# Clustered attention and a mixture of experts on one core: 32-row transposes on VectorE, other operand parts, filler matmuls by plan, and new instruction orders

## The chip, the cores and the metric

The kernel runs on one core of one Trainium2 chip. The metric is device time in microseconds (us), as a median of repeated executions. Engines are named as in the profile: PE (TensorE, matrix products), PEld (its weight loads), DVE (VectorE), ACT (ScalarE), POOL (GpSimd) and SP (SyncE, whose queue issues every DMA of this kernel).

## The reference

Attention in which a query sees only the keys of its own cluster, then a layer in which every token takes the two best of four causal attention experts:

```python
# q, k, v: (4, 8, 768, 64); centroids: (8, 16, 64)
q_assign = np.argmax(np.einsum('bhsd,hcd->bhsc', q_n, c_n), axis=-1)   # q_n, k_n, c_n: rows of length 1
k_assign = np.argmax(np.einsum('bhsd,hcd->bhsc', k_n, c_n), axis=-1)
mask = q_assign[:, :, :, None] == k_assign[:, :, None, :]
scores = np.where(mask, scale * np.matmul(q, k.transpose(0, 1, 3, 2)), -1e9)
attn = np.exp(scores - scores.max(-1, keepdims=True))
x = attn / (attn.sum(-1, keepdims=True) + 1e-9) @ v     # heads side by side: (4, 768, 512)
logits = x @ w_gate                                     # the two best experts of a token, softmax w over them
for e in range(4):
    q, k, v = x @ wq[e], x @ wk[e], x @ wv[e]           # 64 columns each
    ...                                                 # causal softmax attention a
    out += (w where e was chosen) * (a @ v @ wo[e])
```

## The kernel before

The work is cut into 24 pairs `n`. Pairs 0 to 15 are the attention: a batch and two heads each. Pairs 16 to 23 are the experts: a batch and two experts each. A pair has two stages, operands (`attention_operands`, `moe_operands`) and `core`.

Operands of an attention pair. One DMA each brings `kt` and `qt` (L620; the profile shows every DMA at L468; runs of 1536 bytes in a partition). PE turns them in 128x128 blocks against the identity (`misc<-identf,kt`, L633), so that the partition holds the depth of even and of odd tokens, and ACT or DVE copies the result to `xk`, `xq`. They are split into a rounded part `hi` and a rest `lo`, so that products in the fast fp32r format keep their precision. Then the clusters are found:

- PE multiplies by the normalised centroids, four 32-row pieces side by side (L661), and the result (cluster in the partition, token in the column) is copied to `s` (L475).
- PE turns `s` in three 128x128 blocks (L670), so that a token's 16 products lie side by side.
- DVE finds the best of the 16 and makes the one-hot `oh` in five instructions of 384 columns (L676, L677, L678, L683, L684).
- PE turns `oh` back in three blocks (L692), and ACT makes the mask rows `rows` of it, with a scale and a bias that give 0 or -2^60 (L695). They go through DRAM (`rw`) into rows 64 to 79 of `tq` and `tk`.

`tk` and `tq` are the operands of the score products, with two slots of 128 rows each, filled by DMAs on SP (`put`, `put_last`): slot 0 has `hi` of K and of Q and the mask rows, slot 1 the crossing parts (`lo` of K with `hi` of Q, and the other way round). For pairs from 1 on, 63 of the 64 crossing rows lie in slot 1 and one row in row 96 of slot 0.

`core`. For each half of 384 queries: 12 row products per half over an 80-row slot (`row`, L1098; `st` for some of pair 0), of each of which DVE takes the largest element of a row (`mx<-row`, L1109). A small product turns the maxima (`misc<-identr,M`, L1121), ACT or DVE negates them into `mr`, and a DMA writes them as one more row of `tq` (`tq<-mr`, L1145). Then come the scores, two products each (`st`, L1180), the exponential on ACT (L1186), the product with V (`av`, L1225), and the sums of the exponentials, which POOL or DVE adds up (`acc`, L480 and L481) and PE reduces (L1251). 1/sum goes through DRAM to a broadcast tile `rb`, and the result to `xt` and to DRAM (`x`). The experts do the same with projections in place of loads (L857, L907, L1340).

What sets the order. Every step is an `op` with a number. The table `ORDER` lists the numbers for each engine, and `Plan.run` records the instructions in these orders, picking by an estimate of times which engine's next step comes first. So an engine's queue is fixed by the table, and each engine works its queue strictly in order. The table also says which of ACT, DVE and POOL does a copy or a sum that can run on two of them.

Filler. `spin` (L1355) is a product of ones, 256 columns of bf16, into the bank `av`. `Plan.run` puts it into gaps that it expects on PE, but only until the first real use of that bank. All 52 stand before the first `av` product.

Of the kernel before, what the change touches and what calls it, by code (L numbers as in the profile page):

```python
# [1409 lines left out]
```

## Time and profile before

| | us |
|---|---|
| median of 3 runs | 704.73 (704.49 to 705.03) |
| the profiled execution's own time | 706.39 |
| its span, first to last instruction | 704.6 |
| PE busy | 683.0, 97% of the span |
| DVE busy | 536.4, 76% |
| ACT, POOL busy | 396.3 (56%), 339.6 (48%) |
| mean granted PE clock | 0.988 |

The page gives each engine's busy time as a share of the span. A view of windows gives the same for a stretch of time, with the PE clock that was granted there (1.00 is full speed) and the mean share of the 16 DMA engines. A timeline lists instructions with start and duration, and in brackets how long the engine had been idle and what ended that. Matmuls overlap, so what one costs is read from the start of one to the start of the next, not from its duration.

### The profile page before, as it was taken

To read this page: it belongs to the slowest core of one execution; us is meant where nothing else is said; L and a number is where in the kernel's file an instruction comes from. 1 tells how busy PE (TensorE), PEld (TensorE's weight loads), DVE (VectorE), ACT (ScalarE), POOL (GpSimd) and SP (SyncE) were. 2 spreads that over 40 slices of the span, in tenths; PEclk is the share of its full clock that TensorE was granted. 3 is DMA by queue.
4 is the path that set the end of the run, shared out by engine and by line. 5 is a ranking of instruction groups with operands and counts; after the bars stand their busy time and mean duration, and the time that the engine had idled before them with its cause. 6 is when DMAs were issued, how large, how long until landed. Compare 5 with 4: busy or idle time off the path is not lost.

```text
span 704.6 us, 12566 instructions
## 1 busy us (share of the span) xinstructions
PE 683.0 (97%) x4204; PEld 512.4 (73%) x4204; DVE 536.4 (76%) x1127; ACT 396.3 (56%) x938; POOL 339.6 (48%) x281
## 2 busy tenths in 40 slices
PE   6899999999999999999999899989999999999997
PEld 4667667676766677767666588778967888897775
DVE  6898888787988788898788775676678488668842
ACT  6766757666675667757655554345355345343643
POOL 6726577685677356755555521643244101312520
PEclk9999999999999999999999899989999999999999
DMA  6876657567466466567565334253534446234322
GB/s 204 206 189 185 171 139 187 153 170 216 138 204 170 124 193 189 148 184 208 148 186 147 102 99 101 81 158 90 150 81 136 112 123 167 69 99 137 114 99 105
DMA packets 64871, 103.60 MB, mean 147 GB/s; under 512 B 22424, under 2 KB 39080, under 8 KB 64808
## 3 DMA queue, kind: packets, MB, share of 16 engines
q1 hardware_dynamic: 64808, 102.81, 52.9%
q8 instruction: 33, 0.54, 0.3%
q14 instruction: 30, 0.25, 0.1%
HBM read 39.49 MB, written 15.86 MB: 79 GB/s over the span
## 4 chain that ended last, share of the span: by engine, by line
PE 83%; DMA 8%; DVE 4%; ACT 2%; SPq 2%; issue 1%; POOL 1%; DVEq 0%; ACTq 0%
PE st L1180 23%; PE av L1225 20%; PE row L1098 13%; PE misc L857 9%; PE misc L907 5%; PE misc L1340 4%; PE misc L633 3%; PE misc L1251 2%; DMA tq<-mr 2%; DMA r<-sd 2%; SPq L468 2%; DVE acc L481 1%; DVE mx L1109 1%; PE misc L661 1%; DMA sd<-ssb 1%
## 5 line engine op out<-in xcount | busy, mean ns | idle before, releaser
L1109 DVE TENSOR_REDUCE mx<-row 128x1 f32<-128x384 f32 (+1 forms) x442 | 233.5, 549 | 58.9 <-PE row L1098 54.8
L1180 PE MATMUL st<-tq,tk 97*128 97x384 f32 (+4 forms) x1056 | 247.8, 342 | 3.0 <-DMA tq<-mr 1.8
L1180 PEld LDWEIGHTS st<-tq,tk 128*128 128x128 f32 (+1 forms) x1056 | 184.7, 193 | 18.1 <-issue 4.6
L1098 PE MATMUL row<-tk,tq 80*128 80x384 f32 (+3 forms) x506 | 173.0, 366 | 5.4 <-DVE mx L1109 3.7
L1098 PEld LDWEIGHTS row<-tk,tq 80*128 80x128 f32 x506 | 94.5, 193 | 46.7 <-DVE mx L1109 22.5
L1186 ACT ACTIVATE p<-st 128x384 f32<-128x384 f32 (+2 forms) x198 | 89.6, 477 | 58.9 <-PE st L1180 46.9
L1186 ACT ACTIVATE xh<-st 128x384 f32<-128x384 f32 x126 | 59.0, 492 | 35.8 <-PE st L1180 28.4
L1225 PE MATMUL av<-p,vt 128*64 128x384 f32 x308 | 56.4, 493 | 0.0
L1107 DVE TENSOR_TENSOR row<-row,tri 128x128 f32<-128x128 f32 x96 | 28.2, 294 | 34.1 <-PE row L1098 34.0
L1186 ACT ACTIVATE xl<-st 128x384 f32<-128x384 f32 x90 | 42.5, 489 | 14.2 <-PE st L1180 12.0
L480 POOL TENSOR_TENSOR acc<-acc,p 128x768 f32<-128x768 f32 (+1 forms) x18 | 33.2, 1846 | 33.7 <-ACT p L1186 15.9
L1225 PE MATMUL av<-xh,vt 128*64 128x384 f32 x252 | 45.6, 490 | 0.0
L1186 ACT ACTIVATE tk<-st 128x384 f32<-128x384 f32 (+2 forms) x66 | 27.2, 431 | 25.2 <-PE st L1180 24.9
L480 POOL TENSOR_TENSOR acc<-acc,xh 128x768 f32<-128x768 f32 x17 | 31.2, 1837 | 15.9 <-DVE acc L481 9.5
L1225 PEld LDWEIGHTS av<-p,vt 128*64 128x64 f32 x308 | 20.1, 136 | 25.4 <-issue 22.6
L480 POOL TENSOR_TENSOR lo<-xq,hi 128x384 fp32r<-128x384 f32 x23 | 23.6, 1039 | 28.0 <-DMA tk<-lo 17.3
L1302 POOL TENSOR_TENSOR xt<-avu,rb 128x384 f32<-128x384 f32 x28 | 29.0, 1046 | 12.3 <-DMA rb<-rd 9.8
L486 ACT ACTIVATE tk<-hi 64x768 fp32r<-64x768 f32 x39 | 32.8, 841 | 0.9 <-DVE hi L476 0.3
L1109 DVE TENSOR_REDUCE M<-row 128x1 fp32r<-128x512 f32 (+3 forms) x64 | 31.5, 492 | 2.2
L1225 PE MATMUL av<-xl,vt 128*64 128x384 f32 x180 | 33.1, 489 | 0.0
L1225 PEld LDWEIGHTS av<-xh,vt 128*64 128x64 f32 x252 | 17.2, 137 | 21.7 <-issue 21.3
L480 POOL TENSOR_TENSOR lo<-xk,hi 128x384 fp32r<-128x384 f32 x20 | 21.7, 1090 | 22.7 <-DMA tq<-lo 12.8
(300 smaller groups left out, 1381.9 us busy)
## 6 DMA issues: line engine op xcount, KB each, us to landing
tq<-hi SPq DMA_DIRECT2D x62, 192.0 KB
tk<-hi SPq DMA_DIRECT2D x46, 192.0 KB
tq<-lo SPq DMA_DIRECT2D x46, 192.0 KB
rb<-rd SPq DMA_DIRECT2D x46, 192.0 KB
vt<-in_v_dram SPq DMA_DIRECT2D x16, 384.0 KB
x<-xt SPq DMA_DIRECT2D x16, 384.0 KB
kt<-in_k_dram SPq DMA_DIRECT2D x15, 384.0 KB
qt<-in_q_dram SPq DMA_DIRECT2D x15, 384.0 KB
```

Source lines behind the costliest of these rows:

```text
L480: ways = [("pool", t_pool(n), lambda: POOL.tensor_tensor(dst(), a(), b(), op=fn)), ("dve", t_dve(n), lambda: DVE.tensor_tensor(dst(), a(), ...
L486: return op("act", t_act(n, True), lambda: ACT.activation(dst(), src(), AF.Copy), due, after, [use], alt=(MO["m_copy"], "pool", t_pool(n), ...
L857: PE.matmul(m()[:, :HW], w_[:, dc, es], x_[dc]()[:, c], start=(i == 0), stop=(i == 3 * DC - 1))
L907: PE.matmul(m()[:, :NV], x_[dc]()[:, ts], w_[:, dc, :], start=(i == 0), stop=(i == 3 * DC - 1))
L1098: PE.matmul(ps()[:, :w], cols(Q, slice(0, R), 0, h, hf, cc * 128, (cc + 1) * 128), by_head(K)[0:R, 0, h, i * w:(i + 1) * w] if moe else by ...
L1107: DVE.tensor_tensor(e, e, tri, op=OP.add)
L1109: DVE.tensor_reduce(to, ps()[:, :w], axis=AX.X, op=OP.max)
L1180: PE.matmul(p()[:, o_:HW], cols(K, rs, slot, h, kh, k0, k0 + 128), cols(Q, rs, slot, h, hf, o_, HW), start=(i == 0), stop=(i == 1))
L1186: ACT.activation(pt()[:, h, o_:HW], p()[:, o_:HW], AF.Exp, scale=SC)
L1225: PE.matmul(av()[h * 64:(h + 1) * 64, o_:HW], d["vv"](h, kc), pt()[:, h, o_:HW], start=(kc == 0), stop=(kc == nk - 1), tile_position=(0, 6 ...
L1302: e.tensor_tensor(xt().rearrange("d (p c t) -> d t c p", c=HC, t=2)[:, par], avu()[:, c].rearrange("d (c p) -> d c p", c=HC), rb()[:, c].r ...
L1340: PE.matmul(m(), a_()[:, ts], w_()[:, ep, :], start=(ep == 0 and i == 0), stop=(ep == EP - 1 and i == 2))
```

## The change

1. Both turns of the cluster step move from PE to DVE. DVE's transpose works within blocks of 32x32, so the layout is changed to suit it: the operands now have head and depth in the partition (no longer parity and depth), one centroid operand `cbd` for both heads of a pair with zeros where head and row don't match, and 32 rows of products for a piece. The products are turned from PSUM to PSUM (L692 of the new kernel), without the copy `s`; the one-hot `oh` is turned within SBUF to `ot` (L695), and ACT makes the mask rows from it (L714). Pair 0 does the step in two halves of 192 columns and writes its mask rows straight into `tk` and `tq` with ACT (L773), without a DMA.
2. The loads of K and Q become two DMAs each, one for a head, that write runs of 256 bytes. V's token order changes with it.
3. The crossing rows of every pair are now 32 rows in slot 0 and 32 in slot 1 (pair 0 had this before), so `put_last` goes. Counted in the built programs, SP issues 719 DMAs in place of 661: 32 more loads, 30 more operand parts, 4 fewer mask-row writes.
4. The filler has 128 columns, in the unused part of the bank `av`, and may stand anywhere that the plan expects a gap, with a running allowance of 0.7 us. There are 90 of them now: 70 before the first `av` product, 1 in the middle of the attention, 19 among the experts.
5. Constants that aren't needed at once are written later (`late_constants`), and the plan has other estimates for DMAs.
6. `ORDER` is new for all engines.

The same functions run on the engines otherwise. By the built programs DVE has 33 transposes more, and 5 sums of 768 columns, 4 of 384, 5 casts of 384 and 6 copies `ssb` fewer; POOL has 5 sums of 768 and 4 of 384 more.

```diff
-        o = op("pe", t_av(HW), go, c1 + 4, xs["k"] + xs["q"] + [cbd_ready], [m1, s_, x["k"], x["q"]], mode=32)
-        o = copy_op(s_, lambda: m1()[:, :HW], HW, c1 + 4.5, [o], [m1, s_])
...
-                PE.transpose(m2()[:, c * 128:(c + 1) * 128], s_()[:, c * 128:(c + 1) * 128], identf)
+        o = op("dve", t_dve(HW), lambda: DVE.transpose(m2()[:, :HW], m1()[:, :HW]), c1 + 4.5, [o], [m1, m2, oh, sm])
+
+        def turn_back(o, due, dst):
+            return op("dve", t_dve(HW), lambda: DVE.transpose(dst(), oh()), due, [o], [oh, dst])
...
-                PE.transpose(m4()[:, c * 128:(c + 1) * 128], oh()[:, c], identb)
-        o_r = op("act", t_act(HW) + 0.18, lambda: ACT.activation(
-            rows(), m4()[:, :HW], AF.Identity, scale=row_scale, bias=row_bias), c2 + 6.5, [o], [m4, rows])
+            o = turn_back(o, c2 + 3, ot)
+            o_r = op("act", t_act(HW, True) + 0.18, lambda: ACT.activation(
+                rows(), ot(), AF.Identity, scale=row_scale, bias=row_bias), c2 + 6.5, [o, late], [ot, rows])
...
-                dma(t().rearrange("p h c d -> p h (c d)"),
-                    src[b, 2 * pr:2 * pr + 2].rearrange("h (p c) d -> p h (c d)", c=NC))
+                        dma(t().rearrange("p (c h d) -> p h c d", c=NC, h=2)[:, h],
+                            src[b, 2 * pr + h].rearrange("(p c) d -> p c d", c=NC))
...
         for T, src, after in ((K, klo, los["k"]), (Q, qhi, his["q"])):
-            if n:
-                need_st += [put(T, slice(64, 127), 1, src, c2 + 0.8, after), put_last(T, src, c2 + 0.9, after)]
-            else:
-                need_st += [put(T, slice(96, 128), 0, src, c2 + 0.8, after),
-                            put(T, slice(64, 96), 1, src, c2 + 0.9, after, d0=32)]
+            need_st += [put(T, slice(96, 128), 0, src, c2 + 0.8, after),
+                        put(T, slice(64, 96), 1, src, c2 + 0.9, after, d0=32)]
...
-        top, mr_ = (0, 96) if moe else (1, 127 if n else 96)
+        top, mr_ = 0 if moe else 1, 96
...
+    REST, EASE = 0.7, 0.35
...
+                if self.start and not self.held:
+                    gap, dur = t - free["pe"], dur * self.pace(free["pe"])
+                    room = max(0.0, self.REST - self.rest)
...
+                    while mode == 128 and gap > max(room, 0.06) + dur:
                         f = Op("pe", dur, fn, 0.0, (), (), 0.0, 128, None, 0.0, False)
...
+                        self.rest = max(0.0, self.rest - self.EASE * dur)
+                    self.rest += max(gap, 0.0)
...
-        PE.matmul(idle()[:, :256], onesb, onesb[:, None, :].to_broadcast([128, 2, 128]), start=True, stop=True)
+        PE.matmul(avp[:, HW:], onesb, onesb, start=True, stop=True)
...
 ORDER = dict(
     pe="""
-6 4 11 9 1 181 0 18 179 186 20 184 193 23 195 346 56 48 50 54 64 348 46 62 60 52 58 351 66 353 68 74 198 360 80 71 76
+7 5 12 1 10 188 19 186 183 181 349 195 58 76 352 52 347 66 64 48 354 62 56 50 68 60 82 70 54 361 90 73 78 94 92 86 108
...
```

Three places in the queues, first of before and then of the change (a name's number is that of its buffer). The first is PE in the middle of the attention, from the centroid products of a pair (`misc<-xq,cbd`) on; before, PE turns their copy `s` three times a few products later, and `oh` some twenty rows further on.

```order
L661 MATMUL misc_2313<-xq_2170,cbd 32x384
L661 MATMUL misc_2313<-xk_2130,cbd 32x384
...
L1098 MATMUL row_2322<-tk_95,tq_96 128x384
L1180 MATMUL st_2329<-tq_100,tk_99 128x384 x2
L1098 MATMUL row_2335<-tk_95,tq_96 128x384
L670 MATMUL misc_2338<-identf,s_2327 128x128 x3
L1180 MATMUL st_2344<-tq_100,tk_99 128x384 x2
...
L1098 MATMUL row_2424<-tk_95,tq_96 128x384
L692 LDWEIGHTS oh_2411
L692 MATMUL misc_2426<-identb,oh_2411 128x128
...
L1098 MATMUL row_2431<-tk_95,tq_96 128x384
```

The same stretch of PE's queue with the change:

```order
L688 MATMUL misc_2292<-xq_2179,cbd 32x384
L688 MATMUL misc_2292<-xk_2008,cbd 32x384
...
L1129 MATMUL row_2300<-tk_86,tq_87 128x384
L1211 MATMUL st_2304<-tq_91,tk_90 128x384 x2
L1211 MATMUL st_2310<-tq_91,tk_90 128x384 x2
L1129 MATMUL row_2315<-tk_86,tq_87 128x384
L1211 MATMUL st_2317<-tq_91,tk_90 128x384 x2
L1129 MATMUL row_2323<-tk_86,tq_87 128x384
```

Both groups of turns have left PE; row and score products follow each other as before. The second place is DVE in the same pair: before, the two halves of the one-hot step (`sm`, `oh`), with the row maxima (`mx<-row`) and sums around them.

```order
L1109 TENSOR_REDUCE mx_2360<-row_2352 128x1
L1115 TENSOR_REDUCE M_102<-mx_2216 128x6
L676 TENSOR_REDUCE sm_2371<-misc_2338 128x24
L677 TENSOR_TENSOR misc_2338<-misc_2338,sm_2371 128x384
L678 TENSOR_TENSOR misc_2338<-misc_2338,ramp 128x384
L1109 TENSOR_REDUCE mx_2360<-row_2362 128x1
L481 TENSOR_TENSOR lo_2404<-xq_2170,hi_2320 128x384 x2
L481 TENSOR_TENSOR acc_0_2252<-acc_0_2252,p_0_2246 128x768
L683 TENSOR_REDUCE sm_2371<-misc_2338 128x24
L684 TENSOR_TENSOR oh_2411<-misc_2338,sm_2371 128x384
L1109 TENSOR_REDUCE mx_2360<-row_2414 128x1
```

The same step of DVE with the change:

```order
L1140 TENSOR_REDUCE mx_2228<-row_2315 128x1
L692 STREAM_TRANSPOSE misc_2331<-misc_2292 128x384
L1140 TENSOR_REDUCE mx_2228<-row_2323 128x1
L701 TENSOR_REDUCE sm_2345<-misc_2331 128x24
L702 TENSOR_TENSOR misc_2331<-misc_2331,sm_2345 128x384
L703 TENSOR_TENSOR misc_2331<-misc_2331,ramp 128x384
L708 TENSOR_REDUCE sm_2345<-misc_2331 128x24
L709 TENSOR_TENSOR oh_2374<-misc_2331,sm_2345 128x384
L1140 TENSOR_REDUCE mx_2228<-row_2338 128x1
L695 STREAM_TRANSPOSE ot_2380<-oh_2374 128x384
L1140 TENSOR_REDUCE mx_2228<-row_2349 128x1
```

The two transposes stand before and behind the five instructions, and in this pair the two `lo` and the sum that stood between them are no longer there. The third place is PE in the second pair of experts, behind its last projection of Q (`row` and `st` are the row and score products, `M` the maxima, `acc` the sums):

```order
L1098 MATMUL row_6016<-tk_97,tq_98 128x384
L1121 MATMUL misc_6018<-identr,M_102 6x128
L1098 MATMUL row_6022<-tk_97,tq_98 128x384
L1098 MATMUL row_6031<-tk_97,tq_98 128x320
L1251 MATMUL misc_6035<-acc_0_5719,ones_82 32x384
...
L1121 MATMUL misc_6050<-identr,M_102 6x128
L1098 MATMUL row_6060<-tk_95,tq_96 128x512
L1180 MATMUL st_6062<-tq_98,tk_97 128x128 x2
L1180 MATMUL st_6067<-tq_98,tk_97 128x256 x2
```

The same place with the change; of each group of fillers the first is shown (they are 4, 4, 5, 1 and 5):

```order
L1129 MATMUL row_5967<-tk_88,tq_89 128x320
L1392 LDWEIGHTS onesb
L1392 MATMUL av<-onesb 128x128
...
L1152 MATMUL misc_5982<-identr,M_93 6x128
L1129 MATMUL row_5984<-tk_88,tq_89 128x384
L1392 LDWEIGHTS onesb
...
L1283 MATMUL misc_6000<-acc_0_5684,ones_79 32x384
...
L1152 MATMUL misc_6021<-identr,M_93 6x128
L1129 MATMUL row_6023<-tk_86,tq_87 128x128
L1129 MATMUL row_6027<-tk_86,tq_87 128x256
L1211 MATMUL st_6030<-tq_89,tk_88 128x256 x2
```

The products stand in much the same order, and 19 fillers now stand between them.

More of the change, by code (lines that the diff above doesn't have):

```diff
@@ L239, in __init__ @@
             self.ways[alt[1]] = alt[2:]
-        self.start = self.end = None
+        self.start = self.end = self.hold = None
 class Plan:
@@ L345, in run @@
         self.lanes, self.moved = [0.0] * self.LANES, 0.0
+        self.rest, self.start, self.held = 0.0, False, False
         order, mode, place = [], 128, dict.fromkeys(queues, 0)
@@ L371, in run @@
                 t_ = t
-                for issue, move in o.dur:
+                for issue, move, reach in o.dur:
                     t_ = max(t_, self.lanes[0])
-                    self.moved = max(self.moved, t_ + self.REACH) + move
+                    self.moved = max(self.moved, t_ + reach) + move
                     self.lanes = self.lanes[1:] + [self.moved]
@@ L556 @@
     M6 = consts.tile([128, 2, 2, HC], FR)
-    identr = consts.tile([128, 128], FR)
-    DVE.tensor_copy(identr, identf)
     def clear_rows(s):
@@ L624, in attention_operands @@
         x, xs, his, los = {}, {}, {}, {}
         for i, (name, src) in enumerate((("k", k), ("q", q))):
-            t, ld = load(name, src, t0 + AT["load"], 1, name + "t")
-            x[name], xs[name] = work("x" + name, (128, 2, HW)), []
-            for h in range(2):
-                m = misc() if n or name == "k" else plan.buf(psum, "row", (128, 512), FT, 2)
-                def go_t(t=t, m=m, h=h):
-                    for c in range(HC):
-                        PE.transpose(m()[:, c * 128:(c + 1) * 128],
-                                     t()[:, h, 2 * c:2 * c + 2, :].rearrange("p c d -> p (c d)"), identf)
-                due = c1 + 2 * i + h
-                o = op("pe", t_tr(HC), go_t, due, [ld], [t, m, x[name]])
-                xs[name].append(copy_op(lambda xx=x[name], h=h: xx()[:, h], lambda m=m: m()[:, :HW], HW, due + 0.5, [o],
-                                        [m, x[name]]))
+            t, turn = work(name + "t", (128, S)), turned(n, name)
@@ new lines, in attention_operands, with go_t, go @@
+            ld = op("sp", 4 * [(0.64, 0.65, 2.3)] if turn else 2 * [(0.64, 0.85, 2.3)], go, t0 + AT["load"], use=[t])
+            x[name], xs[name] = work("x" + name, (128, 2, HW)), []
+            for hf in range(2):
+                if not turn:
+                    m = misc() if n or name == "k" else plan.buf(psum, "row", (128, 512), FT, 2)
+                    def go_t(t=t, m=m, hf=hf):
+                        for c in range(HC):
+                            PE.transpose(m()[:, c * 128:(c + 1) * 128],
+                                         t()[:, (hf * HC + c) * 128:(hf * HC + c + 1) * 128], identf)
+                    o = op("pe", t_tr(HC), go_t, c1 + 2 * i + hf, [ld], [t, m, x[name]])
+                    xs[name].append(copy_op(lambda xx=x[name], hf=hf: xx()[:, hf], lambda m=m: m()[:, :HW], HW,
+                                            c1 + 2 * i + hf + 0.5, [o], [m, x[name]]))
+                    continue
+                def go(t=t, xx=x[name], hf=hf):
+                    DVE.transpose(xx()[:, hf].rearrange("d (c j u) -> d c u j", c=HC, u=4),
+                                  t().rearrange("p (u f c i) -> p f c u i", u=4, f=2, c=HC)[:, hf])
+                xs[name].append(op("dve", t_dve(HW), go, c1 + 2 * i + hf, [ld], [t, x[name]]))
@@ L739, in attention_operands, with mask, go @@
-            need_row2 = [place_rows(Q, 0, (1,))]
-        def put(T, rs, slot, src, due, after, pars=(0, 1), d0=0):
+            def mask(T, i, par):
+                ot, o = masks[par]
+                def go(e):
+                    for h in range(2):
+                        r = slice(64 * h + 32 * i, 64 * h + 32 * i + NK)
+                        to, src = T[64:64 + NK, 0, h, par], ot()[r]
+                        if e is ACT:
+                            ACT.activation(to, src, AF.Identity, scale=row_scale[r], bias=row_bias[r])
+                        elif i:
+                            DVE.tensor_scalar(to, src, BIG, -BIG, op0=OP.mult, op1=OP.add)
+                        else:
+                            DVE.tensor_copy(to, src)
+                return op("act", 2 * t_act(HW, True) + 0.1, lambda: go(ACT), c2 + 6.6 + par, [o, late] + free, [ot],
+                          alt=(MO["m_copy"], "dve", 2 * t_dve(HW), lambda: go(DVE)), port=True)
@@ L743, in put @@
+            need_row = [mask(K, 1, 0), mask(Q, 0, 0), mask(K, 1, 1)]
+            need_row2 = [mask(Q, 0, 1)]
+        def put(T, rs, slot, src, due, after, hs=(0, 1), d0=0):
             nd = rs.stop - rs.start
             def go():
-                for par in pars:
-                    dma(T[rs, slot, par].rearrange("d h j -> d (h j)"),
-                        src()[par * D + d0:par * D + d0 + nd].rearrange("d h j -> d (h j)"))
-            return op("sp", len(pars) * [(0.66, 0.86 * nd / D)], go, due, after + free, [src])
```

264 lines of the change are left out of this document (144 added, 120 removed), and 321 rows, old and new, of tables (act, dve, pe, pool).

## The prediction

> **What bounds the kernel now.** I read the page first: the span, the busy shares, the shares of the chain that ended last.
>
> ```profile
> span 704.6 us, 12566 instructions
> ...
> PE 683.0 (97%) x4204; PEld 512.4 (73%) x4204; DVE 536.4 (76%) x1127; ACT 396.3 (56%) x938; POOL 339.6 (48%) x281
> ...
> PE 83%; DMA 8%; DVE 4%; ACT 2%; SPq 2%; issue 1%; POOL 1%; DVEq 0%; ACTq 0%
> ```
>
> PE is busy 97% of the span and is 83% of the chain. An average hides stages, so the windows come next (us, PE, PEld, DVE, ACT, POOL busy, granted PE clock, DMA share, GB/s): pairs 2 to 15 of the attention run in 28 to 378, the experts from 405 on.
>
> ```profile
> 28.00:378.00 350.00, 344.86 (x2097) 240.31 (x2097) 292.49 (x559) 230.01 (x528) 214.54 (x152) 1.00 0.64 173
> 405.00:705.00 300.00, 291.76 (x1837) 241.58 (x1833) 200.72 (x481) 135.20 (x344) 91.85 (x99) 0.98 0.40 113
> ```
>
> In the attention PE is idle 5.1 us of 350 at full clock; DVE is second with 84%, DMA has 0.64. The groups of that window say what PE waits for there (busy, mean ns of one, then idle before them and its releasers).
>
> ```profile
> L1098 PE MATMUL row<-tk,tq 80*128 80x384 f32 x333 | 115.6, 368 | 1.9 <-DVE mx L1109 1.5 <-DMA r<-sd 0.2
> ```
>
> The row products, which fill the banks that DVE empties, wait for DVE only 1.5 us in 333 products. So between 28 and 378 time goes by what PE has to do, and work taken off PE there is worth its whole issue time until DVE gets late. A median lies at 704.73, the profiled execution at 706.39; sums are made against the latter and then shifted by −1.66. Differences up to 0.2% (1.4 us) I call no change.
>
> **1. The turns leave PE.** Matmuls overlap, so I take steps from start to start in PE's timeline.
>
> ```profile
> 196.16 0.49 PE L670 MATMUL misc<-identf,s 128*128 128x128 f32 x3
> 196.40 0.42 PE L1098 MATMUL row<-tk,tq 80*128 80x384 f32 x1
> 196.66 0.87 PE L1180 MATMUL st<-tq,tk 97*128 97x384 f32 x4
> 197.37 0.34 PE L1098 MATMUL row<-tk,tq 80*128 80x384 f32 x1
> 197.55 0.34 PE L1180 MATMUL st<-tq,tk 97*128 97x384 f32 x1
> ...
> 202.71 0.34 PE L692 MATMUL misc<-identb,oh 128*128 128x128 bf16 x3
> 202.89 0.50 PE L633 MATMUL misc<-identf,qt 128*128 128x128 f32 x3
> ```
>
> Three f32 turns hold the next product back 196.40 − 196.16 = 0.24 us, and that row product then takes 0.26 to its successor where an ordinary one takes 197.55 − 197.37 = 0.18: 0.32 together. Three bf16 turns take 202.89 − 202.71 = 0.18. That is 0.505 us a pair unrounded, and 14 pairs stand in the PE-bound stage: **−7.1**. It is 0 if another engine is as late; pairs 0 and 1 run beside fillers and give nothing. The copy `s` leaves ACT and DVE too; both have idle time there, so I count nothing for it.
>
> **2. DVE takes them.** No DVE transpose is in the trace. The nearest rows: a copy of 384 columns from PSUM, a cast within SBUF, an in-place pass over the same tile `misc`; the dearest is a pass over 768 columns.
>
> ```profile
> L476 DVE CAST hi<-xk x5: 340/352/361, 6.6 to 311.4; 128x384 fp32r<-128x384 f32 x5
> ...
> L476 DVE COPY s<-misc x3: 547/558/558, 85.8 to 371.8; 128x384 f32<-128x384 f32 x3
> ```
> ```profile
> L481 DVE TENSOR_TENSOR acc<-acc,p 128x768 f32<-128x768 f32 x13 | 12.4, 954 | 0.1
> ...
> L677 DVE TENSOR_TENSOR misc<-misc,sm 128x384 f32<-128x384 f32 x14 | 7.9, 567 | 1.2
> ```
>
> For PSUM to PSUM I take 0.56, nearest to the copy and the pass over `misc`; for bf16 in SBUF 0.5, between the cast's 0.35 and 0.56. Bounds are 0.35 and 0.95 for either. So 28 × 0.53 = +14.8 us, less five sums (5 × 0.954) and five casts (5 × 0.352) that leave DVE: +8.3 on 292.5 in about 343, or 88%. That lies in DVE's idle time unless it makes a bank come free late. Scaling the 1.5 us of waits by the idle share (16% down to 12%) gives +0.5; one row product's step (0.18) lost at each of 28 transposes gives +5. I take **+1** (0 to +5). The moved sums go to POOL (214.5 of 350 busy), whose idle time hides them.
>
> The waits change as well. DVE's queue is strict, so a transpose that waits for the centroid products holds the maxima behind it, and PE's row products behind those. Its forerunner there, the first reduction, waited for PE's turns; its group has 0.0 us of idle time in 14:
>
> ```profile
> L676 DVE TENSOR_REDUCE sm<-misc 128x24 f32<-128x384 f32 x14 | 7.7, 547 | 0.0
> ```
>
> The transpose waits for an earlier step of the same chain (no copy, no turn between), but its row in DVE's queue comes earlier too, a row product and two scores behind the centroid products in the fenced order; PE issues these in about 0.5 us. I count nothing for it; a full miss would hold DVE some 0.5 us, 14 × 0.5 = 7 us of DVE's idle 42. ACT's mask rows now wait for DVE in place of PE; nothing urgent stands behind them, since ACT is busy 230 of 350.
>
> **3. The clock in the second expert pair.** Three stretches ran at about half clock. In the window view:
>
> ```profile
> 390.00:398.00 8.00, 6.70 (x24) 5.03 (x24) 5.31 (x9) 3.98 (x9) 2.01 (x2) 0.58 0.76 208
> 467.40:474.00 6.60, 6.57 (x25) 6.46 (x26) 3.70 (x10) 3.26 (x9) 4.89 (x7) 0.56 0.82 218
> 526.80:532.00 5.20, 5.20 (x28) 2.62 (x29) 1.91 (x6) 1.30 (x6) 4.50 (x4) 0.67 0.60 180
> ```
>
> PE's timeline shows what preceded each, beside a shorter gap after which the clock stayed at full speed (in brackets the idle time and its releaser).
>
> ```profile
> 20.12 0.44 PE L1098 MATMUL st<-tk,tq 80*128 80x384 f32 x1 [0.98 <-DMA tk<-rows]
> ...
> 391.30 0.67 PE L1098 MATMUL row<-tk,tq 80*128 80x384 f32 x1 [1.91 <-DVE mx L1109]
> ...
> 466.08 0.22 PE L1121 MATMUL misc<-identr,M 128*6 128x128 f32 x1 [0.84 <-DVE M L1115]
> 467.43 0.76 PE L1098 MATMUL row<-tk,tq 80*128 80x512 f32 x1 [1.12 <-issue]
> ...
> 526.79 0.22 PE L1121 MATMUL misc<-identr,M 128*6 128x128 f32 x1 [1.18 <-DVE M L1115]
> ```
>
> The three drops follow gaps of 1.91, of 0.84 and 1.12 close together, and of 1.18; one of 0.98 alone passed. The 19 new fillers stand at the second of these. By the next row one of 256 columns takes 1.69/14 = 0.12 us, so one of half the columns about 0.06, and 19 are 1.1 us in gaps of 2.0: no piece left is near 1 us.
>
> ```profile
> 11.30 1.69 PE L1355 MATMUL av<-onesb 128*128 128x256 bf16 x14
> ```
>
> The half-clock stretch then goes: 6.6 × 0.44 = **−2.9** (0 to −2.9). The gaps themselves stay. Nothing is planted at the third; it stays in the sum, and is worth 5.2 × 0.33 = 1.7 plus its gap 1.2 if the new order removes it.
>
> **4. From attention to experts.** Ahead of the gap of 1.91, DVE and POOL did this:
>
> ```profile
> 386.14 4.64 DVE L481 TENSOR_TENSOR acc<-acc,xh 128x768 f32<-128x768 f32 x3
> ```
> ```profile
> 388.13 1.83 POOL L480 TENSOR_TENSOR xl<-vm,xh 128x768 fp32r<-128x768 f32 x1 [5.09 <-ACT xh L475]
> ```
>
> Three sums in a row kept DVE from the maxima, and took 4.64 in place of 3 × 0.954 = 2.9 while POOL worked. Gap and clock cost 1.9 + 8 × 0.42 = 5.3. DVE has five such sums fewer, and its order here is new; no filler stands there. So it may all go or all stay (0 to −5.3); I take half, **−2.6**.
>
> **5. Loads, parts, prologue: 0.** Two transfers followed each other with little else in flight, `rw<-rows` (192 KB in runs of 1536 bytes) and a weight load (128 KB in runs of 256); SP's timeline has their issues, the window view their stretches.
>
> ```profile
> 127.77 0.35 SPq L468 DMA_DIRECT2D rw<-rows  x1
> 128.24 0.38 SPq L468 DMA_DIRECT2D vm<-in_moe_wv_dram  x1
> ```
> ```profile
> 128.50:129.25 0.75, 0.75 (x6) 0.75 (x6) 0.44 (x2) 0.75 (x4) 0.51 (x1) 1.00 0.77 256
> 129.25:130.00 0.75, 0.75 (x8) 0.72 (x6) 0.75 (x2) 0.75 (x4) 0.00 (x0) 1.00 0.75 176
> ```
>
> Scaled to a full share that is 256/0.77 = 332 and 176/0.75 = 235 GB/s, so 384 KB take 1.67 us in place of 1.18, and a pair's two loads 1 us more in 25 at a share of 0.64: hidden, while loads stand a pair ahead; uncovered, 14 us. SP issues 58 DMAs more at 0.59 (first row below, median), 34 us; the second row shows one of its many waits for a releaser, slack that hides them.
>
> ```profile
> L468 SPq DMA_DIRECT2D tq<-hi x108: 461/590/1652, 12.8 to 658.4; - x108
> ```
> ```profile
> SPq L468 <- ACT p L1186: 17.4, 11, 6.3
> ```
>
> In the prologue five transposes (5 × 0.53 = 2.7 us) meet two idle stretches of DVE, 1.61 and 1.21, and the mask rows' DMA of 3.55 leaves the chain:
>
> ```profile
> 11.06 0.56 DVE L676 TENSOR_REDUCE sm<-st 128x24 f32<-128x384 f32 x1 [1.61 <-PE st L670]
> ...
> 15.28 0.72 DVE L731 CAST tk<-rows 16x384 fp32r<-16x384 f32 x2 [1.21 <-ACT rows L695]
> ```
> ```profile
> 16.53 3.55 DMA tk<-rows
> ```
>
> Then DVE's twelve maxima are late next: 0, between −1 and +2.
>
> **Sum:** −7.1 + 1 − 2.9 − 2.6 = −11.6; 706.39 − 11.6 = 694.8 profiled, less 1.66: **693** us.
>
> **Rivals.** *Clock not held.* Fillers and new order leave the half-clock stretches where they are. For it: the stretch ahead of the third drop, below, has PE busy 2.59 of 3.8 us, so an engine busy two thirds of the time lost its clock, and the fillers may not lift the second stretch above that. Against it: the gap of 0.98 passed.
>
> ```profile
> 525.00:528.80 3.80, 2.59 (x15) 1.20 (x14) 1.60 (x5) 2.35 (x6) 3.30 (x3) 0.88 0.51 124
> ```
>
>  Only 1 and 2 are left: −6.1, 698.6. Chance 0.20. The Trainium skill, "TensorE: Matmul & The Clock Gate", Part 1, has the gate close after an idle window of about 3.4 µs, by which pieces of 0.1 us planted in gaps of about 1 us would change nothing and this would be the outcome; the rows disagree, since no gap here is over 1.91 us and the clock fell thrice.
>
> *DVE becomes the bound.* If a transpose takes 0.95, DVE gets 28 × 0.42 = 11.8 us more and stands at 91%; half of that shows: 694.8 + 5.9 − 1.66 = 699. Against it: 1.5 us of waits now. Chance 0.09. By the Trainium skill, "VectorE: DVE Perf Modes", The three transpose paths, VectorE needs 311 ns for 128x128 in bf16, so 0.93 us for three by estimate, which is this rival; no transpose is in the trace to judge it.
>
> *Slower: `mr` behind longer lists on SP.* The maxima's row `tq<-mr` is written on SP, in order, and the scores wait for it. Groups of parts are now four issues long; one more pair of issues ahead of each of 30 writes is up to 2 × 0.59 = 1.2 us. From 11.6/30 = 0.39 us a write on nothing is left; at half, 0.6, it is +18: 711. For it: the 58 issues. Against it: PEld waited for `tq<-mr` only this in 350 us (total, times, longest):
>
> ```profile
> PEld st L1180 <- DMA tq<-mr: 3.2, 4, 1.5
> ```
>
> Chance 0.08.
>
> *It gives nothing.* The freed 7.1 us become waits for the exponential or maxima, in an order that fits no worse and no better: 704. Chance 0.05.
>
> **Numbers.** My forecast has 0.58, and 693 is its sum. Low end: −7.1 − 2.9 − 5.3 − 1.7 − 1.2 − 1 = −19.2, so 685. High end: no clock and DVE at +5, −2.1, so 703. What lies outside is the slower case, most of the one that gives nothing, and tails: under 0.2. Faster: 0.58 + 0.20 + 0.08 = 0.86; same: 0.01 + 0.04 = 0.05; slower 0.08 + 0.01 = 0.09.
>
> **What would show it.** Right: PE busy down by about 7 in the attention and still over 98% of that stage; transposes of 0.5 to 0.56; clock 1.00 behind the second expert pair's row stage; DVE near 88%. Wrong: row products that wait over 5 us for `mx`; drops of the clock with fillers in place; `st` waiting for `tq<-mr` over 10 us; an attention stage that is not shorter.

## The result, and the profile after

The changed kernel took 714.14 us (median of 4 runs, 711.64 to 715.49), the kernel before 704.61 (4 runs, 702.26 to 705.03): ratio 1.0138, 95% interval 1.0098 to 1.0178. It is 9.5 us slower, and 21 us above the forecast of 693. The profiled execution took 715.49 us with a span of 713.4, so 8.8 us more than the span of before. Where an execution took over 1.5% longer than the fastest of its kernel, the medians of `a_long1`, `a_turns` and `a_longpro` below are taken without it.

From the page after: the span, the busy shares, the chain's shares.

```profile
span 713.4 us, 12494 instructions
...
PE 677.6 (95%) x4145; PEld 505.9 (71%) x4145; DVE 542.3 (76%) x1150; ACT 400.4 (56%) x937; POOL 345.9 (48%) x284
...
PE 72%; DMA 13%; DVE 5%; SPq 4%; issue 2%; ACT 2%; POOL 2%; ACTq 0%; POOLq 0%; DVEq 0%
```

PE has 5.4 us less to do and yet ends later; its share of the chain fell from 83 to 72%, DMA's rose from 8 to 13%. The windows of the same stretches:

```profile
0.00:28.00 28.00, 17.28 (x135) 11.44 (x135) 19.77 (x56) 20.39 (x37) 21.28 (x26) 1.00 0.90 196
28.00:378.00 350.00, 333.56 (x1953) 230.37 (x1954) 281.40 (x552) 219.91 (x504) 218.07 (x154) 0.98 0.68 167
```

PE is idle 16.4 us between 28 and 378, where it was idle 5.1, and in the first 28 us the DMA engines are busy 0.90 of the time. The group of row products names the wait:

```profile
L1129 PE MATMUL row<-tk,tq 80*128 80x384 f32 x318 | 111.8, 371 | 12.0 <-DMA tq<-rw 9.5 <-DVE mx L1140 1.5 <-DMA tk<-rw 0.8
```

Before, this row had 1.9 us, 1.5 of it for DVE. Now 10.3 us go to the mask rows, which come through DRAM (`rw`) into `tq` and `tk`. Ahead of the longest of these waits stand these issues in SP's timeline, and this piece in the chain:

```profile
185.07 0.52 SPq L484 DMA_DIRECT2D rw<-rows  x1
185.69 1.33 SPq L484 DMA_DIRECT2D tq<-lo  x2
187.07 0.60 SPq L484 DMA_DIRECT2D rd<-r  x1
187.77 1.28 SPq L484 DMA_DIRECT2D kt<-in_k_dram  x2
189.15 1.05 SPq L484 DMA_DIRECT2D tk<-rw  x2
190.24 0.42 SPq L484 DMA_DIRECT2D vt<-in_v_dram  x1
190.71 0.93 SPq L484 DMA_DIRECT2D tq<-rw  x2
```
```profile
191.22 5.39 DMA tq<-rw
```

The rows were written at 185.07. Two loads of 384 KB, one of K and one of V, were issued ahead of the last fetch of 48 KB, and that fetch took 5.39 us to land. PE's timeline shows the end of it, and three others like it:

```profile
37.75 0.66 PE L1129 MATMUL row<-tk,tq 80*128 80x384 f32 x1 [2.69 <-DMA tq<-rw]
...
67.69 0.41 PE L1129 MATMUL row<-tk,tq 80*128 80x384 f32 x1 [1.25 <-DMA tq<-rw]
...
196.85 0.41 PE L1129 MATMUL row<-tk,tq 80*128 80x384 f32 x1 [3.88 <-DMA tq<-rw]
...
355.50 0.41 PE L1129 MATMUL row<-tk,tq 80*128 80x384 f32 x1 [1.69 <-DMA tq<-rw]
```

What a load costs on SP, in the view of tile `kt` (ns minimum, median, maximum), and the share of the DMA queue on the page (packets, MB, share of 16 engines), before and after:

```profile
L468 SPq DMA_DIRECT2D kt<-in_k_dram x15: 386/473/964, 1.2 to 330.3; - x15
```
```profile
L484 SPq DMA_DIRECT2D kt<-in_k_dram x30: 566/632/701, 1.3 to 355.6; - x30
```
```profile
q1 hardware_dynamic: 64808, 102.81, 52.9%
```
```profile
q1 hardware_dynamic: 113616, 102.72, 56.2%
```

One issue of 473 ns became two of 632, and nearly the same bytes move in 1.75 times as many packets. Where the 8.8 us lie is read from the first and last start of the products with V (`p` with `vt` in the attention, with `vm` among the experts):

```profile
L1225 PE MATMUL av<-p,vt x308: 486/486/537, 32.0 to 458.0; 128*64 128x384 f32 x154
L1225 PE MATMUL av<-p,vm x88: 272/486/603, 475.4 to 688.5; 128*64 128x384 f32 x56, 128*64 128x128 f32 x16, 128*64 128x256 f32 x16
```
```profile
L1256 PE MATMUL av<-p,vt x308: 486/486/902, 39.3 to 466.2; 128*64 128x384 f32 x154
L1256 PE MATMUL av<-p,vm x88: 272/486/537, 481.6 to 697.9; 128*64 128x384 f32 x56, 128*64 128x128 f32 x16, 128*64 128x256 f32 x16
```

The first such product comes 7.3 us later (39.3 for 32.0). From there to the last it is 2.1 longer (658.6 for 656.5), and what follows is 0.6 shorter. Not all of the 7.3 is lost: 3 row and 6 score products more now stand ahead of that first product, 9 × 0.18 = 1.6 us by the prediction's step. Single executions are read here; the same instructions can differ by some 4 us between two of them (`a_nofill` below).

The change places its fillers a little otherwise than stated above: the trace has 69 ahead of the first product with V, 1 in the attention (at 133.3) and 20 among the experts.

### The profile page after: what moved, and what is told of

Its sections match the earlier page's. It is cut to its first block, busy times and chain, and to the rows that moved or that the text cites. A ratio compares the mean times of both kernels' runs of the same rounds, so it can differ in the third digit from the quotient of the medians.

```text
span 713.4 us, 12494 instructions
## 1 busy us (share of the span) xinstructions
PE 677.6 (95%) x4145; PEld 505.9 (71%) x4145; DVE 542.3 (76%) x1150; ACT 400.4 (56%) x937; POOL 345.9 (48%) x284
## 4 chain that ended last, share of the span: by engine, by line
PE 72%; DMA 13%; DVE 5%; SPq 4%; issue 2%; ACT 2%; POOL 2%; ACTq 0%; POOLq 0%; DVEq 0%
PE st L1211 20%; PE av L1256 17%; PE row L1129 11%; PE misc L888 8%; PE misc L938 5%; PE misc L1372 4%; SPq L484 4%; DMA tq<-rw 2%; PE misc L652 2%; PE misc L1283 2%; DMA tq<-hi 1%; POOL acc L496 1%; DMA tq<-mr 1%; DVE acc L497 1%; DMA rb<-rd 1%
## 5 line engine op out<-in xcount | busy, mean ns | idle before, releaser
L1211 PE MATMUL st<-tq,tk 97*128 97x384 f32 (+3 forms) x1056 | 246.2, 340 | 4.3 <-ACT tq L1217 1.6
L1129 PE MATMUL row<-tk,tq 80*128 80x384 f32 (+4 forms) x506 | 172.6, 363 | 15.1 <-DMA tq<-rw 9.5
L1256 PE MATMUL av<-p,vt 128*64 128x384 f32 x308 | 59.5, 509 | 0.0
L496 POOL TENSOR_TENSOR acc<-acc,p 128x768 f32<-128x768 f32 (+1 forms) x20 | 35.6, 1778 | 43.6 <-DVE acc L497 30.4
L496 POOL TENSOR_TENSOR lo<-xq,hi 128x384 fp32r<-128x384 f32 x29 | 29.1, 1016 | 29.3 <-ACT hi L491 17.8
L1334 POOL TENSOR_TENSOR xt<-avu,rb 128x384 f32<-128x384 f32 x26 | 26.6, 1032 | 31.0 <-DMA rb<-rd 17.0
L491 ACT ACTIVATE hi<-misc 128x384 fp32r<-128x384 f32 x25 | 12.3, 493 | 49.6 <-PE misc L888 30.5
L502 ACT ACTIVATE tk<-hi 64x768 fp32r<-64x768 f32 x42 | 35.4, 843 | 1.3 <-DVE hi L492 0.4
L1217 ACT ACTIVATE tk<-st 128x384 f32<-128x384 f32 (+2 forms) x66 | 27.3, 431 | 14.6 <-PE st L1211 14.2
L1140 DVE TENSOR_REDUCE M<-row 128x1 fp32r<-128x128 f32 (+3 forms) x64 | 31.4, 491 | 2.2
```

The costliest lines, as they stand in the source:

```text
L496: ways = [("pool", t_pool(n), lambda: POOL.tensor_tensor(dst(), a(), b(), op=fn)), ("dve", t_dve(n), lambda: DVE.tensor_tensor(dst(), a(), ...
L502: return op("act", t_act(n, True), lambda: ACT.activation(dst(), src(), AF.Copy), due, after, [use], alt=(MO["m_copy"], "pool", t_pool(n), ...
L1129: PE.matmul(ps()[:, :w], cols(Q, slice(0, R), 0, h, hf, cc * 128, (cc + 1) * 128), by_head(K)[0:R, 0, h, i * w:(i + 1) * w], start=True, s ...
L1140: DVE.tensor_reduce(to, ps()[:, :w], axis=AX.X, op=OP.max)
L1211: PE.matmul(p()[:, o_:HW], cols(K, rs, slot, h, kh, k0, k0 + 128), cols(Q, rs, slot, h, hf, o_, HW), start=(i == 0), stop=(i == 1))
L1217: ACT.activation(pt()[:, h, o_:HW], p()[:, o_:HW], AF.Exp, scale=SC)
```

## The experiments

The theory: the loads in 256-byte runs, two DMAs each, hold SP and the DMA engines too long, and what stands behind them lands late ("runs"). The rivals: the new list of SP puts loads in bad places ("order"), or the 30 added part DMAs are the cause ("parts"). Differences between two altered kernels are taken between medians.

**Runs of 1536 bytes, two DMAs (`a_long2`) and one (`a_long1`).**

```diff
-                        dma(t().rearrange("p (c h d) -> p h c d", c=NC, h=2)[:, h],
-                            src[b, 2 * pr + h].rearrange("(p c) d -> p c d", c=NC))
+                        dma(t().rearrange("p (h c) -> p h c", h=2)[:, h],
+                            src[b, 2 * pr + h].rearrange("(p c) d -> p (c d)", c=NC))
```

> The changed kernel with the loads of K and Q in runs of 1536 bytes again, still two DMAs each; the blocks that PE turns then hold other tokens and heads, so the attention is computed on mixed-up data (all instructions stay). Theory 'runs': the 256-byte loads hold the DMA engines and SP too long, so the mask rows land late; PE's idle time ahead of row products on DMA tq<-rw and tk<-rw (10.3 us of 350 in 28 to 378) falls under 3 us and the time comes to 702 to 706. Rival 'order': the new list of SP puts loads between the write of the mask rows and their fetch; a load that is only 0.5 us shorter changes little, 710 to 714. Rival 'parts': 30 more part DMAs on SP; 712 to 714.

> As the run before, with one DMA per load in place of two (blocks mixed up in the same way). Theory 'runs': 699 to 704, the fewer issues give 1 to 3 us more. Rival 'order': 708 to 713. Rival 'parts': 711 to 714.

`a_long2` took 709.59 us, ratio to before 1.0056 (1.0025 to 1.0088); `a_long1` 705.4, 1.0009 (0.9972 to 1.0046). So long runs give 4.5 us back, clear of noise, and the single DMA 4.2 more, where the intervals overlap; 8.8 together. Both kernels compute on mixed-up data. The row groups of `a_long2` and of `a_long1`:

```profile
L1129 PE MATMUL row<-tk,tq 80*128 80x384 f32 x329 | 115.5, 371 | 9.7 <-DMA tq<-rw 8.5 <-DVE mx L1140 1.0
```
```profile
L1129 PE MATMUL row<-tk,tq 80*128 80x384 f32 x324 | 114.4, 372 | 7.1 <-DMA tk<-lo 2.3 <-DMA tq<-rw 1.9 <-DMA tk<-hi 1.5
```

In `a_long2` PE still waited 8.5 us for mask rows, where the theory wanted under 3: the time fell and that wait hardly did. In `a_long1` it fell from 10.3 to under 3, and 3.8 us for other parts came up in its place. So the loads' runs cost time, but it isn't shown that they cost it through the mask rows.

**Loads moved behind the fetch (`a_fetch`).** The edit re-sorts SP's list only.

```diff
+        for after, moved in (
+                (203, (18,)),
+                (369, (854, 194)),
...
+                    order.insert(j, order.pop(i))
```

> The changed kernel with SP's list edited alone: in 13 pairs the 19 loads (K, Q, V, weights, x) that stand just ahead of the write of the mask rows or between it and their fetch are moved behind the fetch; the computation is the reference's. Theory 'runs': the loads still take as long and collide elsewhere, 708 to 713. Rival 'order': the fetch lands on time, idle time on tq<-rw and tk<-rw under 3 us, 702 to 706. Rival 'parts': 711 to 714.

719.11 us, 1.0215 (1.0174 to 1.0255): 5 us slower than the change by the medians, and not faster. The fetch lands on time, as rival "order" had it: no row product waits for `rw` between 28 and 378 any more. But now the scores wait 7.7 us for the maxima's rows, where it was 1.3, so the 702 to 706 of that rival falls. The theory's 708 to 713 was too good as well: the wait moved from one small transfer to another.

```profile
L1232 PE MATMUL st<-tq,tk 128*128 128x384 f32 x624 | 154.0, 350 | 8.8 <-DMA tq<-mr 7.7 <-ACT xh L1238 0.8 <-ACT p L1238 0.2
```

**The loads alone on the kernel before (`b_short`).**

```diff
-                dma(t().rearrange("p h c d -> p h (c d)"),
-                    src[b, 2 * pr:2 * pr + 2].rearrange("h (p c) d -> p h (c d)", c=NC))
+                for h in range(2):
+                    dma(t().rearrange("p h c d -> p (h c d)").rearrange("p (c h d) -> p h c d", c=NC, h=2)[:, h],
+                        src[b, 2 * pr + h].rearrange("(p c) d -> p c d", c=NC))
```

> The kernel before with one part of the change alone: each load of K and Q as two DMAs in runs of 256 bytes (its blocks then hold mixed-up tokens and heads, all instructions stay). Theory 'runs': 4 to 10 us slower than before, with waits of PE for mask rows or K and Q. Rival 'order': within 2 us of before, since the old list of SP has the room. Rival 'parts': within 1.5 us of before.

716.50 us, 1.0168 (1.0132 to 1.0203): 12.5 us slower, more than the whole change. Here the late transfers are the maxima's rows, 5.5 us where it was 1.8. In the profiled execution the first product with V comes at 36.9, 4.9 later than before, with 3.4 us at half clock ahead of it. The second line is the DMA queue's on the page:

```profile
L1185 PE MATMUL st<-tq,tk 97*128 97x384 f32 (+1 forms) x627 | 156.4, 350 | 7.1 <-DMA tq<-mr 5.5 <-ACT p L1191 1.0 <-ACT xl L1191 0.3
```
```profile
q1 hardware_dynamic: 106280, 102.81, 54.4%
```

54.4% of this span of 714.7 us is 389 us of all 16 engines, 16 more than before (52.9% of 704.6).

**Loads on ACT's queue (`a_actq`).**

```diff
-                            src[b, 2 * pr + h].rearrange("(p c) d -> p c d", c=NC))
+                            src[b, 2 * pr + h].rearrange("(p c) d -> p c d", c=NC), ACT)
```

> The changed kernel with the 64 load DMAs of K and Q issued by ACT in place of SP, at the same places of the plan; the computation is the reference's. Theory 'queue' (the 256-byte loads cost through SP's strict queue and through what lands behind them in its ring): mask rows, parts and maxima no longer stand behind them, 704 to 709. Rival 'engines' (the 16 DMA engines are held 24 us longer whatever queue issues): 711 to 715. Rival 'ACT' (64 issues of 0.65 us make the exponentials late): 717 or more.

728.25 us, 1.0332 (1.0293 to 1.0372), as rival "ACT" had it. PE still waited 4.4 us for `tq<-rw` and 2.8 for `tk<-rw`, so moving the issue did not free the transfers here; whether the queue or the 16 engines weigh more stays open.

**One crossing row for 32 (`a_parts3`), both together (`a_long1p3`), long runs in the first three pairs (`a_longpro`), and the parts alone on the kernel before (`b_parts`).**

```diff
-            need_st += [put(T, slice(96, 128), 0, src, c2 + 0.8, after),
+            need_st += [put(T, slice(96, 128), 0, src, c2 + 0.8, after, one=n > 2),
```

> The changed kernel with, from pair 3 on, one row by one DMA in place of the 32 crossing rows of slot 0 (two DMAs): 26 DMAs fewer, and 31 crossing rows of each operand are left out. Theory 'runs': at most 3 us faster than the changed kernel, 711 to 714. Rival 'parts' (the 30 more part issues on SP are the cause): 703 to 708.

> The changed kernel with loads as before the change (one DMA each, runs of 1536 bytes, on mixed-up data) and, from pair 3 on, one row by one DMA for the 32 crossing rows of slot 0 (31 rows left out). If both DMA costs add: 701 to 704. If they are the same waits counted twice: 705 to 707.

> The changed kernel with K and Q of pairs 0 to 2 alone loaded as before the change (one DMA each, runs of 1536 bytes; these pairs compute on mixed-up data). If the short runs cost mostly in the prologue, where the DMA engines are 90% busy: 707 to 709. If they cost evenly along the attention: 711 to 713.

> The kernel before with the third part of the change alone: all crossing rows as 32 and 32, two DMAs each in place of two and one (30 DMAs more on SP), the row of the maxima in row 96; the computation is the reference's. If SP's issues are hidden, as the prediction's step 5 had it: within 1.5 us of before. If each added issue delays what stands behind it: 2 to 5 us slower, with more waits for tq<-mr and for parts.

`a_parts3`: 710.46 us, 1.0085 (1.0043 to 1.0126), 3.7 less than the change, a little more than "runs" and much less than "parts" allowed. It moves fewer bytes, and its interval overlaps that of the change, so the 3.7 are not clear of noise. `a_long1p3`: 703.52, 0.9988 (0.9953 to 1.0022), 10.6 less than the change, which is clear. That lies where "both costs add" had it, but it is only 1.9 below `a_long1`, so how far the parts add to the loads stays open. `a_longpro`: 713.6, 1.0122 (1.0072 to 1.0173), no gain that can be told, outside both expectations. Its mean clock is 0.980 to 0.983 where the change has 0.987 to 0.992, with 10 us at half clock between 22 and 33, so it can't say what the first pairs' loads cost. `b_parts`: 703.71, 0.9982 (0.9953 to 1.0011): in the old queue the 30 issues are hidden.

PE's idle time between 28 and 378 goes with the times of these versions better than any one wait does. In one profiled execution each it is 16.4 us in the change, 14.2 in `a_parts3`, 12.2 in `a_long2`, 11.9 in `a_long1`, 5.4 in `a_long1p3` and 19.0 in `a_fetch`. The products with V in `a_long1p3`, and a window of its prologue:

```profile
L1259 PE MATMUL av<-p,vt x308: 486/486/581, 39.8 to 456.5; 128*64 128x384 f32 x154
L1259 PE MATMUL av<-p,vm x88: 272/486/537, 471.9 to 688.4; 128*64 128x384 f32 x56, 128*64 128x128 f32 x16, 128*64 128x256 f32 x16
```
```profile
20.40:37.50 17.10, 16.39 (x70) 13.00 (x71) 11.64 (x24) 11.27 (x23) 6.06 (x6) 0.50 0.86 203
```

From first to last it is 648.6 us, 7.9 less than before, 1.6 of it the products that moved ahead. It starts 7.8 later, but this execution ran 17.1 us at half clock before that start, so its prologue can't be compared with the others.

**PE work put back (`a_turns`).**

```diff
+            if n > 1:
+                for _ in range(3):
+                    PE.transpose(m1()[:, HW:], x["q"]()[:, 0, :128], identf)
+                for _ in range(3):
+                    PE.matmul(m1()[:, HW:], onesb, onesb, start=True, stop=True)
```

> The changed kernel with PE work as long as the removed turns put back behind the centroid products of pairs 2 to 15 (three f32 turns and three 128-column bf16 products into unused columns; results unchanged). If PE bounds the attention, as the prediction's step 1 had it: +7 us, 719 to 723. If PE now waits for late DMAs, part of it falls into waits: +2 to +4.5, 716 to 718.5.

722.1 us, 1.0270 (1.0207 to 1.0333): 8.0 us more than the change in medians, 5.7 between the two profiled spans, whose mean clocks are alike (0.987 and 0.988). So the late DMAs absorb little of the added PE work: they are waits of their own, mostly on top of it.

**The turns alone on the kernel before (`b_dve`, `b_dvep`).** PE's turns and the copy are gone, SP's list is unchanged. In `b_dve` the turned products lie in SBUF, in `b_dvep` in PSUM as in the change.

```diff
-        o = copy_op(s_, lambda: m1()[:, :HW], HW, c1 + 4.5, [o], [m1, s_])
...
+            o = op("dve", t_dve(HW), lambda: DVE.transpose(m1()[:, :HW], m1()[:, :HW]), c1 + 4.5, [o], [m1, s_])
...
+                DVE.transpose(ot(), oh().rearrange("p a b -> p (a b)"))
```

> The kernel before with the first part of the change alone, from pair 1 on: DVE turns the products (from PSUM into s, in place of the copy) and the one-hot rows; loads, parts, list of SP and fillers stay as they were; the computation is the reference's. If the removed PE work is worth its issue time as the prediction's step 1 had it: 14 x 0.505 less, 696 to 699. Rival 'DVE becomes the bound': 701 to 704. Rival 'the chain to the mask rows gets later': 705 or more.

> The kernel before with the first part of the change alone, from pair 1 on, the one-hot passes in PSUM as in the change: DVE turns the products in place in their bank and the one-hot rows in SBUF; PE's turns and the copy s are gone, loads, parts, SP's list and the expert stage are as before; the computation is the reference's. Step 1 of the prediction: 696 to 699. Rival 'DVE becomes the bound, its new waits for the centroid products hold the maxima': 702 to 708. Rival 'turns on DVE as such are the loss': 712 or more.

`b_dve`: 733.83 us, 1.0416 (1.0354 to 1.0479). It tested something else as well: its two-operand passes, 0.57 us each in PSUM, came to medians of 1.03 and 1.24 in SBUF (view of tile `s`).

```profile
L680 DVE TENSOR_TENSOR s<-s,sm x15: 557/1032/2153, 17.1 to 405.6; 128x384 f32<-128x384 f32 x15
L681 DVE TENSOR_TENSOR s<-s,ramp x15: 557/1244/2067, 18.2 to 406.2; 128x384 f32<-128x384 f32 x15
```

`b_dvep` has that cost away: 709.62 us, 1.0076 (1.0041 to 1.0111), still 5 us slower than before. Its window from 28 to 378 and its waits, then the wait of the weight loads before:

```profile
28.00:378.00 350.00, 341.11 (x1993) 233.20 (x1991) 298.56 (x573) 222.86 (x511) 211.16 (x150) 0.99 0.62 171
```
```profile
PEld row L1105 <- DVE mx L1116: 22.4, 43, 1.5
PE row L1105 <- DVE mx L1116: 3.1, 6, 1.2
```
```profile
PEld row L1098 <- DVE mx L1109: 17.1, 30, 1.1
```

This fits the prediction's rival with DVE as the bound, though DVE is busy only 85%: in an order made for turns on PE, transposes delay the maxima for which the row products wait. It is argued, not shown: no run gave DVE more room in that order. The waits for the maxima's rows grew too, and the median clock of its runs is 0.988 where the kernel before had 0.993 beside it, so part of the 5 us is half clock behind such waits.

**Fillers (`a_nofill`, `b_dve_fill`, `b_dvep_fill`, `b_fill`, `b_fill3`).**

```diff
+                    pad = {(16, 1): (8, 6), (18, 1): (8, 0)}.get((n, hf), (0, 0))
+                    for _ in range(pad[0]):
+                        PE.matmul(m()[:, 256:384], onesb, onesb, start=True, stop=True)
...
+                        for _ in range(16 if (n, hf, kc, h) == (14, 0, 0, 1) else 0):
+                            PE.matmul(p()[:, HW:], onesb, onesb, start=True, stop=True)
```

> The changed kernel without its 20 later fillers (one in the attention, 19 among the experts); all other work stays. The prediction's step 3: the clock falls to half behind the second expert pair's row stage (around 470 to 482), and the time rises by about 3 us, to 717. Rival (fillers there do nothing): no stretch of half clock there, within 1.5 us of 714.

> The run before with 22 fillers of 128 columns around the two gaps of the experts' row stages that ended at 466 to 467 and at 527 in the kernel before, written into unused columns of the bank of the maxima. If a filled gap keeps the clock: no half clock at these two places, 3 to 5 us less than the run before, 692 to 695. If not: within 1.5 us of the run before.

> The run before with the 22 fillers around the two gaps of the experts' row stages. If filled gaps keep the clock: 2 to 5 us less than the run before and no half clock at the two places. If not: within 1.5 us of it.

> The kernel before with nothing but 22 fillers of 128 columns around the two gaps of the experts' row stages that end at 466 to 467 and at 527, in unused columns of the bank of the maxima; the computation is the reference's. Step 3 of the prediction (a filled gap keeps the clock): no half clock at 467 and 527, and 2.9 + 1.7 = up to 4.6 us less than before, 699.5 to 702. Rival (the clock falls anyway): within 1.5 us of before.

> The run b_fill with 16 more fillers (about 1 us) in the gap of 1.9 us that ended at 391 in the kernel before, in unused columns of a score bank; the computation is the reference's. If the half-clock stretch behind that gap is the gap's doing: no half clock at 391 to 398, 1.5 to 3.5 us less than b_fill, 697.5 to 699.5. If not, or if the fillers hold up the scores behind them: within 1 us of b_fill or slower.

The stretch of the second gap in the change, and the same place in `a_nofill`:

```profile
464.00:482.00 18.00, 16.82 (x112) 12.56 (x110) 16.97 (x51) 8.50 (x20) 8.09 (x8) 1.00 0.68 197
```
```profile
480.50:487.30 6.80, 6.58 (x25) 6.11 (x24) 4.97 (x13) 3.35 (x10) 4.49 (x6) 0.50 0.62 194
```

With the fillers the clock stays at 1.00; without them, behind a gap of 0.86 us, it is 0.50 for 6.8 us, 3.4 us lost. `a_nofill` took 723.78 us, 1.0254 (1.0204 to 1.0304), 9.6 more than the change, but about half of that can't be the fillers' doing. By its trace the attention's filler is still there (at 132.8) and so is one of the experts': 19 are left out, all behind 472 us. Yet its last product with V of the attention already starts 4.1 us later than that of the change (470.3 for 466.2), after the same instructions, with 10 us more at half clock on the way. The mean clock of its four runs is 0.975 to 0.979 for 0.987 to 0.992; why the clock fell more often there stays open.

`b_dve_fill`: 733.11 us (1.0398, 1.0350 to 1.0446), no step from `b_dve` that could be told, a miss. The half clock behind the first gap is gone from its trace, but there is more of it in the attention instead. `b_dvep_fill`: 707.56 (1.0056, 1.0029 to 1.0083), 2.1 less than `b_dvep`, with intervals that overlap. `b_fill`: 701.09, 0.9958 (0.9936 to 0.9980), 2.9 less than before. With `b_fill3` it is the only version whose interval lies below the kernel before. Its windows at the two gaps:

```profile
463.00:470.00 7.00, 7.00 (x48) 5.89 (x48) 6.06 (x15) 5.81 (x15) 5.64 (x8) 1.00 0.86 220
520.00:528.00 8.00, 7.06 (x47) 5.15 (x47) 5.55 (x17) 5.41 (x14) 6.81 (x5) 1.00 0.68 198
```

`b_fill3` filled the gap at 391 as well: 701.18, 0.9971 (0.9948 to 0.9993), the same as `b_fill`. Behind its gap, now 0.91 us, the clock held:

```profile
395.46 0.45 PE L1098 MATMUL row<-tk,tq 80*128 80x384 f32 x1 [0.91 <-DVE mx L1109]
```
```profile
395.00:402.00 7.00, 6.54 (x37) 4.29 (x38) 5.42 (x11) 5.09 (x11) 4.05 (x3) 1.00 0.70 194
```

Its profiled execution lost the clock elsewhere instead, and the time did not fall.

## Why the prediction was wrong, step by step

**Step 5 failed first, in its overlap.** It priced loads and part DMAs at nothing because DMA stood at 0.64 and SP had waits to spare, and named 14 us if that cover was gone. The price was near: 16 us more of the engines in `b_short`, where 32 loads at the step's 0.49 make 15.7. The cover was not there. The loads alone cost 12.5 us on the kernel before and 8.8 within the change; the parts perhaps 3.7 more, which is not clear of noise, and nothing in the old queue. The average share and the sum of slack said nothing of a transfer that PE waits for: a 48 KB fetch behind two loads landed 5.39 us after its issue. The rival of `mr` behind longer lists on SP was the nearest, 711, and its mechanism holds for the loads alone (`tq<-mr` 5.5 us in `b_short`); in the change itself `st` waited only 1.3 us for `mr`, and the mask rows, which are written, read back and then wanted, took its part. Which small transfer is late changes with the order of SP (`a_fetch`).

**The prologue failed with it.** It was put at 0 (−1 to +2). The first product with V comes 7.3 us later, of which 1.6 is work that moved ahead of it. Part of the rest is the short loads': alone on the kernel before they make it 4.9 later (`b_short`). Part is not: with long runs in the change 4.7 are left (`a_long1`), 1.6 of them moved work. Which of the new orders, the two-half step or the loads' places makes that part was not tried.

**Step 1 had the mechanism, and not its condition.** Turns of that length cost about their issue time when put back (5.7 to 8.0 us for 7.0). But taking them off PE in the old order lost 5 us in place of winning 6. The step's bound "0 if another engine is as late" was the case; the reading that PE waits only 1.5 us for DVE left out the weight loads, which waited 17.1 us for the same maxima. That this wait was the sign to read is argued, not shown.

**Step 2.** The durations were right: 0.591 and 0.567 us by the groups after, for 0.56 and 0.5.

```profile
L692 DVE STREAM_TRANSPOSE misc<-misc 128x384 f32<-128x384 f32 x13 | 7.7, 591 | 1.1 <-PE misc L688 0.6 <-ACT ssb L1289 0.5
...
L695 DVE STREAM_TRANSPOSE ot<-oh 128x384 bf16<-128x384 bf16 x13 | 7.4, 567 | 0.1
```

The Trainium skill, "VectorE: DVE Perf Modes", The three transpose paths, has 311 ns for 128x128; three times that, 0.93 by the prediction's estimate, is not what the rows show for 384 columns. The price of +1 (0 to +5) was mis-sized: against the −7.1 of step 1, `b_dvep` leaves about +12 in the old order. What it is in the new order no run shows alone.

**Step 3 was right**, by its own working: the half clock at that place returns when the fillers are taken out, and fillers alone gain 2.9 us (interval 1.4 to 4.5) for two such gaps, of which 2.9 was forecast for one. The rival in which the clock isn't held falls there.

**Step 4.** The gap at 391 and its half clock are gone in the change (27.0 of 27 us busy at full clock in 378 to 405), as the step allowed at most. A filled gap kept the clock in `b_fill3` as well, without a gain that can be measured.

```profile
378.00:405.00 27.00, 27.00 (x164) 18.46 (x163) 24.01 (x45) 18.05 (x41) 18.34 (x13) 1.00 0.61 170
```

But four other stretches of half clock came, two behind waits for mask rows (2.69 and 3.88 us) and two behind waits for ACT (1.71 and 1.57). They are 17 us in all, as in before, so the clock gave nothing in sum:

```profile
36.90:43.70 6.80, 5.95 (x18) 2.85 (x20) 2.21 (x5) 1.89 (x4) 1.81 (x2) 0.50 0.81 206
197.40:200.80 3.40, 3.40 (x14) 3.02 (x13) 2.21 (x5) 2.31 (x5) 0.00 (x0) 0.50 0.68 145
245.20:248.60 3.40, 3.40 (x13) 3.40 (x12) 1.55 (x4) 2.42 (x7) 2.56 (x2) 0.50 0.02 6
...
542.10:545.50 3.40, 3.40 (x18) 3.40 (x17) 2.11 (x6) 0.60 (x3) 1.72 (x2) 0.50 0.01 4
```

**The sum.** From −11.6 to +9.5 are 21.1 us. Loads and parts make 10.6 of them (`a_long1p3`), the slowdown and a little more. The other 10.5 are gains that did not come, and they are not assigned in full. By estimate about half is the clock: the runs of `a_long1p3` have a median of 0.985 where the kernel before had 0.993 beside them, and 0.008 of 703.5 is 5.6 us, if PE bound all the time. Step 1's missing gain and the later prologue lie in the rest.

## What to carry to other kernels

A share of DMA time is no price for a transfer: find the small transfer that an engine waits for, and ask what is issued ahead of it. Work taken off the busiest engine is worth its time only if the engine that takes it has room at the places where the first one waits for it (argued here from `b_dvep`); look at the waits of the weight loads too. Before two executions are compared stage by stage, compare their granted clocks there: the same instructions came out 4 us apart. Price each part of a change alone where it can be built alone: here three parts cost on the kernel before 12.5, 5 and 0 us, and a fourth gained 2.9.
